# RWKV attention and a top-1 mixture of experts in one kernel: the start of the first chunk, and when the first experts' weights are loaded and split

## Chip, cores and metric

The kernel runs on one core of a Trainium2 chip. The metric is the device time of one execution in microseconds (us); three runs of the kernel before took 287.07, 287.21 and 288.65 us.

## What is computed

```python
# attention: 4 batches, 8 heads, 768 tokens, 48 elements a head
for t in range(S):
    kv = einsum('bhd,bhe->bhde', kt, vt)
    y[:, :, t] = einsum('bhd,bhde->bhe', rt, state + u[None, :, :, None] * kv)
    state = wt[..., None] * state + kv
x = y as (3072 tokens, 384)
# experts: 8 of them, 384 -> 1024 -> 384, each token goes to one
skip = x @ w_skip > 0            # which tokens are computed at all
e = argmax(x @ w_gate)           # its expert, gate = softmax weight of that expert
out = x + gate * (relu(x @ w1[e]) @ w2[e])     # for the tokens computed, else x
```

All is float32; matrix products in the expert part are made of two parts per weight, a high part (rounded, "h") and a low part (the weight less the high part, "l").

## The kernel before

**Attention.** The 4 x 768 tokens are 24 chunks of 128 tokens. One loop, `for s in range(-2, n + 1)` (L672), is software-pipelined: step s loads chunk s+4 (`load_chunk`, L168), loads the transposed and the plain v of chunk s+3 (`load_turned`, `load_v`), stores the rows of chunk s-1, prepares chunk s+2, makes the scores of chunk s+1 and the outputs of chunk s. The buffers `wrk_sb` hold w, r and k of a chunk, three of them in turn.

Preparing a chunk: `prep_scan` (L300) makes q, a reverse running product of w, on VectorE (DVE); `prep_keys` (L322) a reciprocal on DVE and kq = k q on GpSimd (POOL); `prep_reads` (L328) a forward scan rh on DVE and rp = r rh, on POOL but for chunk 0, where DVE does it (L335). `bonus_keys` (L317) makes rk = r k on POOL, for chunk 0 at the end of step -2. The scan of rh takes its start values from a table, `reads_w`, that DVE builds at L261. `scores` (L353) are TensorE (PE) matmuls of kq and rp into two PSUM banks psA; `mask` (L362) multiplies them by a triangle into asb on DVE; `outputs` (L405, L409) multiply asb by v. `fill` (L666) issues matmuls on constant data whose result nobody reads, 11 before the loop, 4 at step -1 and 3 at step 0.

In the start, the memsets and small copies to PSUM zeros, to the gate matrices `wgp` and to `ubk` are issued by `setup` (L238), on ScalarE (ACT) and POOL.

**Queues.** All loads and stores of the loop are issued by SyncE (SP) in program order. A DMA signals one of eight semaphores, taken in turn over all DMAs of SyncE and ScalarE; a DMA waits until the DMA eight places earlier, whose semaphore it takes, has landed.

**Experts' weights.** `load_weights(e, q)` (L75) loads the first (q = 0) or second (q = 1) weights of expert e in three DMAs of 512 KB into a buffer of one of two tags. Expert 1's first and second weights and expert 0's second take turns in one of them, `r1`. Splitting a slice of 512 columns is a copy to the high part on ACT and a subtraction for the low part, on POOL (`split_high`, L100, whose subtraction is issued behind the next rp) or on DVE (`split_slice`, L91). In the loop, `parts` and `gens` (L671, L749) say when: expert 0's second weights are loaded at steps 5, 6 and 7 and split from step 7 on, expert 1's first loaded at steps 16 to 18 and split from step 18 on, most of them after step 21; expert 0's first at steps 19 to 21, used unsplit.

**After the loop.** `early_expert` (L639) runs the first 128 tokens of expert 0; h0l is the low part of its hidden layer. `expert(e)` (L853) does the rest of expert 0 and then experts 1 to 7, 256 tokens at most each: hidden layer psH, hh (high part, ACT), hl (low part, DVE), products psO with w2h and w2l, then fin. Between the activations it splits the next expert's weights, one slice at a time (`more`). `tokens` gathers the tokens of the next expert and makes xTh and xTl of them. The second weights of expert 1 (`r_11`) are loaded when the buffer of its first is read to the end.

## Time and profile before

| | us |
|---|---|
| median of the runs (287.07, 287.21, 288.65) | 287.21 |
| the profiled execution | 286.06 |
| its span in the profile | 284.2 |
| PE busy | 271.2 |
| DVE busy | 217.0 |
| ACT busy | 159.4 |
| POOL busy | 145.9 |

The span runs from the first to the last instruction of the trace; the execution's time has 1.86 us more around it. Busy shares are means over stages with different limits, so the rows below are read by stretch. In a row of the timeline the bracket at the end gives how long the engine stood idle before it and what it waited for.

### The profile page before, as it was taken

The numbers are of one execution on the slowest core, as the hardware profiler recorded it, in microseconds if no ns is written. First come the engines' busy times: TensorE is split into PE (matmuls) and PEld (weight loads), VectorE is DVE, ScalarE is ACT, GpSimd is POOL, SyncE is SP. The second block draws the span as 40 slices with busy tenths as digits, with TensorE's granted clock in tenths as the row PEclk, the third lists the DMA queues.
The fourth block names the chain that finished last, engine by engine and source line by source line (L and its number), as shares of the span: only waits on it lengthen the run. The fifth ranks groups of instructions, "written<-read, shape, count | busy, mean of one in ns | idle before, by whom it ended". The sixth has DMA issues, their size and how long they took to land.

```text
span 284.2 us, 8967 instructions
## 1 busy us (share of the span) xinstructions
PE 271.2 (95%) x3601; PEld 248.9 (88%) x3602; DVE 217.0 (76%) x414; ACT 159.4 (56%) x464; POOL 145.9 (51%) x140
## 2 busy tenths in 40 slices
PE   6998999999999999999999999999999999999993
PEld 2687878788887888887999999999999999999992
DVE  7997999999989999972747697948859588595320
ACT  5175555787658957768416573827638276381310
POOL 4986775699978998974656625011030110201111
PEclk9999999999999999999999999999999999999999
DMA  7999999998999869992078997565672656700001
GB/s 217 239 311 333 277 345 339 363 332 246 297 278 302 252 218 348 308 310 65 28 256 294 345 314 267 212 213 200 221 258 68 231 200 221 268 5 28 10 5 41
DMA packets 26131, 64.41 MB, mean 227 GB/s; under 512 B 4342, under 2 KB 15386, under 8 KB 26080
## 3 DMA queue, kind: packets, MB, share of 16 engines
q1 hardware_dynamic: 23712, 58.14, 62.3%
q0 software_dynamic: 2048, 5.48, 5.9%
q8 instruction: 30, 0.49, 0.7%
q10 hardware_dynamic: 320, 0.13, 0.2%
q14 instruction: 21, 0.17, 0.2%
HBM read 56.69 MB, written 7.86 MB: 227 GB/s over the span
## 4 chain that ended last, share of the span: by engine, by line
PE 57%; POOL 8%; issue 6%; DVE 4%; ACT 3%; DMA 1%; POOLq 0%; DVEq 0%; ACTq 0%
PE psH L884 7%; PE psH L883 7%; PE psH L882 7%; PE psO L906 6%; PE psO L908 6%; PE psO L907 6%; PE psH L133 4%; PE psY L409 3%; POOL rp L336 2%; PE psA L358 2%; POOL kq L326 2%; PE psY L413 2%; PE psX L815 2%; PE psO L658 2%; PE psX L425 1%
## 5 line engine op out<-in xcount | busy, mean ns | idle before, releaser
L820 POOL DMA_INDIRECT out<-fin,ids x16 | 16.8, 1047 | 99.1 <-DVE fin L915 92.7
L889 ACT ACTIVATE hh<-psH 128x256 fp32r<-128x256 f32 x60 | 23.1, 385 | 56.6 <-PE psH L884 53.4
L884 PE MATMUL psH<-xTh,w1l 128*128 128x256 f32 x168 | 47.5, 283 | 0.0
L883 PE MATMUL psH<-xTl,w1h 128*128 128x256 f32 x168 | 47.5, 283 | 0.0
L882 PE MATMUL psH<-xTh,w1h 128*128 128x256 f32 x168 | 47.5, 283 | 0.0
L906 PE MATMUL psO<-w2h,hh 128*128 128x384 f32 x120 | 40.9, 341 | 0.0
L908 PE MATMUL psO<-w2h,hl 128*128 128x384 f32 x120 | 40.2, 335 | 0.0
L907 PE MATMUL psO<-w2l,hh 128*128 128x384 f32 x120 | 40.1, 335 | 0.0
L894 DVE SCALAR_TENSOR_TENSOR hl<-psH,hh 128x256 fp32r<-128x256 f32 x60 | 25.1, 418 | 13.3 <-ACT hh L889 12.0
L326 POOL TENSOR_TENSOR kq<-wrk,q 128x512 f32<-128x512 f32 x24 | 28.2, 1177 | 11.7 <-DVE q L309 3.5
L364 DVE TENSOR_TENSOR asb<-psA,c_sb 128x512 f32<-128x512 f32 x48 | 30.4, 676 | 3.5 <-PE psA L358 3.4
L331 DVE TENSOR_TENSOR_SCAN rh<-wrk,rowsk,pss 128x520 f32<-128x520 f32 x24 | 31.1, 1296 | 2.0
L318 POOL TENSOR_TENSOR rk<-wrk 128x512 f32<-128x512 f32 x24 | 31.0, 1292 | 2.4 <-DMA wrk<-wrk 2.4
L884 PEld LDWEIGHTS psH<-xTh,w1l 128*128 128x128 f32 x168 | 32.2, 192 | 0.0
L883 PEld LDWEIGHTS psH<-xTl,w1h 128*128 128x128 f32 x168 | 32.2, 192 | 0.0
L882 PEld LDWEIGHTS psH<-xTh,w1h 128*128 128x128 f32 x168 | 32.2, 191 | 0.0
L309 DVE TENSOR_TENSOR_SCAN q<-wrk,pss 128x520 f32<-128x520 f32 x24 | 29.5, 1230 | 3.0 <-DMA wrk<-wrk 0.9
L336 POOL TENSOR_TENSOR rp<-wrk,rh 128x512 f32<-128x512 f32 x23 | 27.2, 1181 | 5.4 <-DVE rh L331 5.0
L89 DVE TENSOR_TENSOR w2l<-r,w2h 128x512 fp32r<-128x512 f32 x42 | 27.7, 685 | 2.0 <-ACT w2h L88 1.4
L409 PE MATMUL psY<-asb,v 128*48 128x128 f32 x384 | 26.5, 276 | 2.6 <-DVE psY L381 2.3
L915 DVE SCALAR_TENSOR_TENSOR fin<-psO,gates,xg 128x384 f32<-128x384 f32 x15 | 9.3, 618 | 25.2 <-PE psO L908 24.6
L358 PE MATMUL psA<-rp,kq 64*64 64x128 f32 (+1 forms) x768 | 26.0, 251 | 1.8 <-issue 1.1
(154 smaller groups left out, 608.4 us busy)
## 6 DMA issues: line engine op xcount, KB each, us to landing
r<-w SPq DMA_DIRECT2D x48, 512.0 KB
wrk<-wrk SPq DMA_DIRECT2D x21, 772.5 KB
v<-vN SPq DMA_DIRECT2D x24, 192.0 KB
vt<-wrk SPq DMA_DIRECT2D x48, 96.0 KB
out<-x SPq DMA_DIRECT2D x24, 192.0 KB
wrk<-wrk SPq DMA_DIRECT2D x1, 579.4 KB
wrk<-wrk SPq DMA_DIRECT2D x1, 512.0 KB
wrk<-wrk SPq DMA_DIRECT2D x1, 384.0 KB
```

Of the source, the lines that this page charges most:

```text
L318: nc.gpsimd.tensor_tensor(work[i]["rk"].rearrange("p a j -> p (a j)"), t[:, R_OFF:K_OFF], t[:, K_OFF:V_OFF], op=ALU.mult)
L326: nc.gpsimd.tensor_tensor(kq, wk["k"], wk["q"][:, :, 1:1 + P], op=ALU.mult)
L331: nc.vector.tensor_tensor_scan(rh.rearrange("p a j -> p (a j)"), wk["w"][:, 0:NP * CW], reads_at[:, :NP * CW], rowsk, op0=ALU.mult, op1=AL ...
L336: eng.tensor_tensor(rp, wk["r"], rh[:, :, :P], op=ALU.mult)
L358: nc.tensor.matmul(psa[g][j:j + HP, a, j:], wk["kq"][rows, a, j:j + HP], wk["rp"][rows, a, j:], start=True, stop=True)
L409: nc.tensor.matmul(y_at(a, g), v[:, 2 * a + g], wk["asb"][g][:, a], start=False, stop=True, skip_group_check=True)
L882: nc.tensor.matmul(ps, w1h[:, o:o + P], xTh[:, kc], start=(kc == 0), stop=False)
L883: nc.tensor.matmul(ps, w1h[:, o:o + P], xTl[:, kc], start=False, stop=False)
L884: nc.tensor.matmul(ps, w1l[:, o:o + P], xTh[:, kc], start=False, stop=(kc == KC - 1))
L906: nc.tensor.matmul(pso, h[j, fc][0], w2h[:, o], start=(fc == 0), stop=False)
L907: nc.tensor.matmul(pso, h[j, fc][0], w2l[:, o], start=False, stop=False)
L908: nc.tensor.matmul(pso, h[j, fc][1], w2h[:, o], start=False, stop=(fc == FC - 1))
```

## The change

Chunk 0's transfer of r and k is made in two, k first. Its rp goes from DVE to POOL, and rk of chunks 0 and 1 behind rp. The table of the reads is made by ACT, the constants that ACT spreads come behind it, in a function of their own, after chunk 0's first preparation. Seven of the matmuls that only fill become two. All weights are loaded in six pieces of 512 columns (256 KB). Expert 0's second weights come one piece at a time in six steps, and are split in six named steps; expert 1's first weights are loaded in steps 22 to 24 and split after the loop, their low parts on DVE.

```diff
@@ load_weights
-        for i in range(3):
-            o = i * 1024
-            yield nc.sync.dma_start(wr[:, o:o + 1024],
-                                    w12[e, :, q * KC * DF + o:q * KC * DF + o + 1024])
+        for i in range(6):
+            o = i * 512
+            yield nc.sync.dma_start(wr[:, o:o + 512],
+                                    w12[e, :, q * KC * DF + o:q * KC * DF + o + 512])
@@ load_chunk, i == 0
-                nc.sync.dma_start(t[KO:LO, R_OFF:V_OFF], rows[:2 * D, R_OFF:V_OFF])
+                nc.sync.dma_start(t[KO:LO, K_OFF:V_OFF], rows[:2 * D, K_OFF:V_OFF])
+                nc.sync.dma_start(t[KO:LO, R_OFF:K_OFF], rows[:2 * D, R_OFF:K_OFF])
@@ setup
-            nc.vector.tensor_scalar(reads_w.bitcast(U32), ints, rowsk, None, op0=ALU.mult)
...
+        def spread_constants():
             for z in psa:
                 nc.scalar.copy(z.rearrange("p a j -> p (a j)"), warm)
...
             nc.scalar.copy(ubk_sb, u_sb.rearrange("p (a o) -> p a o", o=1).to_broadcast([P, NP, D]))
@@ prep_scan
-            if i > 0:
+            if i == 0:
+                nc.scalar.activation(reads_w.bitcast(U32), ones_w.bitcast(U32), AF.Copy, scale=rowsk)
+            if i > 1:
                 bonus_keys(i)
@@ prep_reads
-            eng = nc.gpsimd if i > 0 else nc.vector
-            eng.tensor_tensor(rp, wk["r"], rh[:, :, :P], op=ALU.mult)
+            nc.gpsimd.tensor_tensor(rp, wk["r"], rh[:, :, :P], op=ALU.mult)
+            if i <= 1:
+                bonus_keys(i)
@@ the loop
-            parts = [(4, 0, i) for i in range(6, 12)] + [(15, 1, 0)] + [(19, 1, i) for i in range(1, 6)]
+            fetch = {5: (0, 1), 6: (0, 1), 8: (0, 1), 9: (0, 1), 13: (0, 1), 15: (0, 1)}
+            fetch.update({t: (0, 0) for t in (19, 20, 21)})
+            fetch.update({t: (1, 0) for t in (22, 23, 24)})
+            parts = {t: 6 + i for i, t in enumerate((7, 11, 12, 13, 18, 21))}
...
-                    if s == 0:
-                        fill(3)
...
+                if s == -2:
+                    spread_constants()
...
                 if s == -2:
-                    bonus_keys(0)
-                    nc.gpsimd.memset(vt_sb[3], 0.0)
+                    nc.scalar.copy(vt_sb[3].rearrange("p o j -> p (o j)"), warm)
+                if s == -1:
...
-                        fill(4)
+                        fill(2)
...
+                if s in fetch:
+                    eq = fetch[s]
+                    if eq not in gens:
                         gens[eq] = load_weights(*eq)
+                    for _ in range(1 if eq == (0, 1) else 2):
                         next(gens[eq])
+                if s in parts:
+                    split_high(0, parts[s])
@@ after the loop, ahead of expert 0's remainder
-            early_low(1)
+            early_low(2)
+            for i in range(3):
+                split_slice(1, i)
             for k in range(done[0], 6 * FC - 4):
                 next(todo)
             early_tokens(1)
+            for i in range(3, 6):
+                split_slice(1, i)
```

Lines behind the edits have other numbers in the changed kernel (L336 is L338, L318 is L321, L161 is L160, L84 is L83, L89 is L88, L894 is L901). POOL's order at the start, from its last memset of `setup` to rp of chunk 1, before (L717 to L720 are memsets; wrk_88 and wrk_89 are chunks 0 and 1):

```order
L266 MEMSET wgp_sb 128x420
L326 ISA
L326 TENSOR_TENSOR kq_182<-wrk_88,q_178 128x512
L318 TENSOR_TENSOR rk_180<-wrk_88 128x512
L717 MEMSET vt_94 128x512
L718 MEMSET onesb 128x128
L719 MEMSET ohs 128x8
L720 MEMSET key 128x54
L318 TENSOR_TENSOR rk_206<-wrk_89 128x512
L326 TENSOR_TENSOR kq_209<-wrk_89,q_204 128x512
L336 TENSOR_TENSOR rp_213<-wrk_89,rh_211 128x512
```

The same stretch in the changed kernel:

```order
L263 MEMSET wgp_sb 128x420
L329 ISA
L329 TENSOR_TENSOR kq_183<-wrk_88,q_171 128x512
L338 TENSOR_TENSOR rp_187<-wrk_88,rh_185 128x512
L321 TENSOR_TENSOR rk_173<-wrk_88 128x512
L329 TENSOR_TENSOR kq_206<-wrk_89,q_202 128x512
L338 TENSOR_TENSOR rp_210<-wrk_89,rh_208 128x512
L321 TENSOR_TENSOR rk_204<-wrk_89 128x512
```

rp of chunk 0 is new on POOL; rk of chunks 0 and 1 stands behind rp, and the memsets behind both chunks.

SyncE's order at the start, from the second part of chunk 1's load to the load of chunk 2 (wrk_90), with the semaphores waited for (DMAHW0 to 7 are the eight), before:

```order
L180 DMA wrk_89<-wrk 128x1024
L185 DMA v_137<-vN 128x384 [waits DMAHW0_49]
L161 DMA vt_91<-wrk 48x2x256 [waits DMAHW1_49,Pool_49]
L161 DMA vt_91<-wrk 48x2x256 [waits DMAHW2_49]
L180 DMA wrk_90<-wrk 128x1545 [waits DMAHW3_49]
```

And in the changed kernel:

```order
L180 DMA wrk_89<-wrk 128x521
L180 DMA wrk_89<-wrk 128x1024 [waits DMAHW0_49]
L185 DMA v_138<-vN 128x384 [waits DMAHW1_49]
L160 DMA vt_91<-wrk 48x2x256 [waits DMAHW2_49,Pool_49]
L160 DMA vt_91<-wrk 48x2x256 [waits DMAHW3_49]
L180 DMA wrk_90<-wrk 128x1545 [waits DMAHW4_49]
```

With one DMA more in front, each takes the semaphore of the next in the row: the second transposed load of v now waits for DMAHW3 (the second of three small copies of u on ScalarE's queue), for which the load of chunk 2 waited before.

DVE's order between the low parts of the early expert and the first low part of expert 0's remainder (hl_0), in the changed kernel; before, the six rows of w1l are not there, and gates follows h0l:

```order
L640 TENSOR_TENSOR h0l<-hf_2634,h0h 128x512
L640 TENSOR_TENSOR h0l<-hf_2693,h0h 128x512
L88 TENSOR_TENSOR w1l_1_2710<-r_10_2548,w1h_1_2709 128x512 [waits DMAHW7_49,Activation_49]
L88 TENSOR_TENSOR w1l_1_2710<-r_10_2548,w1h_1_2709 128x512 [waits DMAHW0_49,Activation_49]
L88 TENSOR_TENSOR w1l_1_2710<-r_10_2548,w1h_1_2709 128x512 [waits DMAHW2_49,Activation_49]
L88 TENSOR_TENSOR w1l_1_2710<-r_10_2548,w1h_1_2709 128x512 [waits DMAHW3_49,Activation_49]
L88 TENSOR_TENSOR w1l_1_2710<-r_10_2548,w1h_1_2709 128x512 [waits DMAHW5_49,Activation_49]
L88 TENSOR_TENSOR w1l_1_2710<-r_10_2548,w1h_1_2709 128x512 [waits DMAHW6_49,Activation_49]
L790 TENSOR_REDUCE gates<-pss 128x16 [waits PE_49]
L901 SCALAR_TENSOR_TENSOR hl_0_2799<-psH_0_2797,hh_0_2798 128x256 [waits DMAHW4_49,DMAHW1_49,Activation_49]
```

SyncE's order at the end of the attention, from the last load of expert 0's first weights (r_00) to the first load of expert 1's second weights (r_11), before:

```order
L84 DMA r_00_2259<-w 128x1024 [waits DMAHW1_49]
L435 DMA out<-x_2478 128x384 [waits DMAHW2_49,Activation_49]
L435 DMA out<-x_2558 128x384 [waits DMAHW3_49,Activation_49]
L435 DMA out<-x_2594 128x384 [waits DMAHW4_49,Activation_49]
L84 DMA r_11_2760<-w 128x1024 [waits DMAHW5_49,DMASW1_49,Pool_49]
```

And in the changed kernel, from the fourth piece of expert 1's first weights (r_10) on:

```order
L83 DMA r_10_2548<-w 128x512 [waits DMAHW3_49]
L439 DMA out<-x_2586 128x384 [waits DMAHW4_49,Activation_49]
L83 DMA r_10_2548<-w 128x512 [waits DMAHW5_49]
L83 DMA r_10_2548<-w 128x512 [waits DMAHW6_49]
L83 DMA r_11_2764<-w 128x512 [waits DMAHW3_49,DMAHW5_49,DMAHW2_49,DMAHW6_49,DMAHW0_49,DMAHW7_49,DMASW1_49,DVE_49]
```

The first load of r_11 waited for POOL, which had read the last of expert 1's first weights there; it now waits for DVE, which reads them in the six rows of w1l.

## Rows read from the trace of the kernel before

**Rows 1.** The page, part 1: busy time, share of the span and instructions.

```profile
PE 271.2 (95%) x3601; PEld 248.9 (88%) x3602; DVE 217.0 (76%) x414; ACT 159.4 (56%) x464; POOL 145.9 (51%) x140
```

**Rows 2.** Busy time by stretch; the first line names the columns.

```profile
core 0: us, PE busy (x) PEld busy (x) DVE busy (x) ACT busy (x) POOL busy (x), PEclk, DMA share, GB/s
8.00:14.00 6.00, 5.68 (x105) 3.94 (x109) 5.90 (x9) 0.96 (x4) 6.00 (x9) 1.00 0.94 229
...
24.00:60.00 36.00, 34.01 (x707) 29.17 (x705) 33.10 (x56) 22.37 (x82) 25.96 (x23) 1.00 1.03 329
...
84.00:106.00 22.00, 20.62 (x445) 17.80 (x442) 20.66 (x36) 16.19 (x55) 21.25 (x20) 1.00 0.83 256
...
127.00:152.00 25.00, 24.48 (x290) 22.62 (x287) 12.72 (x39) 12.51 (x34) 14.08 (x13) 1.00 0.40 138
152.00:266.00 114.00, 114.00 (x817) 113.72 (x816) 83.13 (x165) 62.71 (x140) 24.56 (x23) 1.00 0.58 203
```

**Rows 3.** Timeline, DVE at the start: start us, us, engine, line, operation, tiles.

```profile
3.52 0.36 DVE L261 TENSOR_SCALAR pss<-pss,rowsk 128x131 uint32<-128x131 uint32 x1
4.00 1.24 DVE L309 TENSOR_TENSOR_SCAN q<-wrk,pss 128x520 f32<-128x520 f32 x1
...
5.49 1.30 DVE L331 TENSOR_TENSOR_SCAN rh<-wrk,rowsk,pss 128x520 f32<-128x520 f32 x1
6.82 1.30 DVE L336 TENSOR_TENSOR rp<-wrk,rh 128x512 f32<-128x512 f32 x1
8.04 1.22 DVE L309 TENSOR_TENSOR_SCAN q<-wrk,pss 128x520 f32<-128x520 f32 x1
...
10.73 1.26 DVE L364 TENSOR_TENSOR asb<-psA,c_sb 128x512 f32<-128x512 f32 x2
...
12.59 1.24 DVE L309 TENSOR_TENSOR_SCAN q<-wrk,pss 128x520 f32<-128x520 f32 x1
...
17.31 1.24 DVE L309 TENSOR_TENSOR_SCAN q<-wrk,pss 128x520 f32<-128x520 f32 x1
...
22.87 1.24 DVE L309 TENSOR_TENSOR_SCAN q<-wrk,pss 128x520 f32<-128x520 f32 x1 [0.93 <-DMA wrk<-wrk]
```

**Rows 4.** Timeline, POOL at the start: kq of chunk 0, rp of chunk 1, rk of chunk 3.

```profile
6.40 1.17 POOL L326 TENSOR_TENSOR kq<-wrk,q 128x512 f32<-128x512 f32 x1 [3.37 <-DMA wrk<-wrk]
...
12.31 1.18 POOL L336 TENSOR_TENSOR rp<-wrk,rh 128x512 f32<-128x512 f32 x1
...
17.34 1.27 POOL L318 TENSOR_TENSOR rk<-wrk 128x512 f32<-128x512 f32 x1 [0.35 <-DMA wrk<-wrk]
```

**Rows 5.** Timeline, SyncE's issues of the loads of chunks 2 and 3.

```profile
5.98 0.35 SPq L180 DMA_DIRECT2D wrk<-wrk  x1
...
12.54 0.35 SPq L180 DMA_DIRECT2D wrk<-wrk  x1
```

**Rows 6.** Groups by line, POOL from 23 to 127 us: low parts, count, busy us, mean ns.

```profile
L107 POOL TENSOR_TENSOR w2l<-r,w2h 128x512 fp32r<-128x512 f32 x6 | 7.6, 1273 | 0.0
```

**Rows 7.** Waits of DVE (8 to 127 us) and PE (8 to 152): total us, times, longest.

```profile
DVE asb L364 <- PE psA L358: 1.1, 3, 0.5
DVE q L309 <- DMA wrk<-wrk: 0.9, 1, 0.9
```

```profile
PE psA L358 <- issue: 1.1, 1, 1.1
...
PE psA L358 <- POOL rp L336: 0.3, 1, 0.3
```

**Rows 8.** The page, part 5: low parts on DVE among the experts.

```profile
L89 DVE TENSOR_TENSOR w2l<-r,w2h 128x512 fp32r<-128x512 f32 x42 | 27.7, 685 | 2.0 <-ACT w2h L88 1.4
```

**Rows 9.** Timeline, the handover: DVE's and ACT's rows, then PE's, then SyncE's load.

```profile
142.84 1.29 DVE L636 TENSOR_TENSOR h0l<-hf,h0h 128x512 fp32r<-128x512 f32 x2
...
147.93 0.42 DVE L894 SCALAR_TENSOR_TENSOR hl<-psH,hh 128x256 fp32r<-128x256 f32 x1 [1.26 <-DMA r<-w]
...
153.22 1.01 DVE L89 TENSOR_TENSOR xTl<-psX,xTh 128x384 fp32r<-128x384 f32 x2
...
142.16 0.21 ACT L574 CAST vals<-pss 128x6 bf16<-128x6 f32 x1
144.91 0.48 ACT L629 COPY xT<-psX 128x384 f32<-128x384 f32 x1 [2.54 <-PE psX L628]
147.51 0.38 ACT L889 ACTIVATE hh<-psH 128x256 fp32r<-128x256 f32 x1 [2.12 <-DMA r<-w]
149.12 0.62 ACT L88 CAST w2h<-r 128x512 fp32r<-128x512 f32 x1 [1.22 <-DMA r<-w]
...
151.78 0.42 PE L906 MATMUL psO<-w2h,hh 128*128 128x384 f32 x1
...
156.15 0.28 PE L883 MATMUL psH<-xTl,w1h 128*128 128x256 f32 x1
...
143.82 13.05 SPq L84 DMA_DIRECT2D r<-w  x9
```

More of the change, by code (lines that the diff above doesn't have):

```diff
@@ L273, in setup @@
             nc.scalar.copy(ubk_sb, u_sb.rearrange("p (a o) -> p a o", o=1).to_broadcast([P, NP, D]))
-            for g in range(2):
-                nc.tensor.matmul(psy2[:, g].rearrange("p s j -> p (s j)"), warm[:, :P], warm,
-                                 start=True, stop=True, skip_group_check=True)
-            nc.tensor.matmul(psu.rearrange("p a j -> p (a j)"), warm[:, :P], warm[:, :NP * HP],
-                             start=True, stop=True, skip_group_check=True)
         later, held, marks, ending = deque(), [], deque(), []
```

20 lines of the change are left out of this document (7 added, 13 removed).

## The prediction

> **What bounds the kernel now.** I read the page's busy shares first, then the table by stretch, then the start of the program instruction by instruction, then the waits of the middle, and last the place where the attention steps hand over to the experts. The page names TensorE (PE) as the busiest engine, 271.2 of 284.2 us [rows 1], but that is an average over unlike stages. The table by stretch [rows 2] shows them: from 152 to 266 us PE is busy 114.00 of 114.00 us, so what is late at 152 is late at the end, and nothing before it is made good there. Between 24 and 106 VectorE (DVE) has almost no slack (33.10 of 36 and 20.66 of 22 us), GpSimd (POOL) is full only from 84 to 106 (21.25 of 22), and the DMA engines are saturated from 8 to 60 (shares 0.94 to 1.03). So there are three questions: when the first steps get their data, who paces the middle, and whether the handover to expert 1 stays hidden.
>
> **The start.** In the rows of DVE [rows 3] look at what stands between the scan q of chunk 0 and asb of chunk 0 at 10.73. The change takes two instructions out of it: the table (0.36 us) and the product rp (1.30 us). It moves the first to ScalarE, which is idle there, and the second to POOL. q of chunk 0 can't start much earlier than 4.00, since its weights must land, so the table is worth 0.1 us at most. After the reciprocal and rh end at 6.78, q of chunk 1 starts at 6.8 instead of 8.04 and asb of chunk 0 at 10.73 - 1.2 = 9.5 to 9.6. PE's scores must be there by then: now kq starts at 6.40, after 3.37 us of waiting for r and k in one transfer [rows 4]. With k first, kq starts when q ends, near 5.3, and ends near 6.5; rp on POOL follows rh, 6.8 to 8.0 by the usual 1.18 us. DVE's rp ended at 8.12. The scores therefore start within 0.2 us of where they do, asb can begin at 9.6, and the first outputs come **1.1 us earlier** (1.66 us at the very most, both instructions whole).
>
> That gain does not survive the next loads. q of chunk 2 starts at 12.59 [rows 3], 0.05 us after the load of chunk 3 was issued at 12.54 [rows 5]; that issue waits for the landing of chunk 2's load (its buffer is another one; the wait is for the DMA eight issues earlier), so chunk 2 had landed just before. POOL waits for chunk 3's landing until 17.34 [rows 4] and q of chunk 3 starts at 17.31; q of chunk 4 waits 0.93 us for its own load, until 22.87 [rows 3]. Three loads in a row are the clock of this stretch, and the DMA engines are saturated from 8 us on [rows 2]. The change doesn't issue them earlier: chunk 2's load is behind one DMA more, and the second transposed v load ahead of it on SyncE's queue now waits for a later one of the eight (the second small copy of u, which landed just before 5.98; before, that wait stood at chunk 2's own load [rows 5]). So it is issued at 6.0 to 6.5 instead of 5.98. The queue is full then, so I take 0 for it and +0.4 as the bad end. The good end is the whole 1.1 us, if chunk 4's load moves with chunk 3's. **Front: 0, from -1.1 to +0.4.** The zero is covered by the loads; DVE waits longer at q of chunk 2 and of chunk 4 instead.
>
> Five fill matmuls go. They run on PE between its scores and the outputs, where PE waits anyway, 5.68 of 6.00 us busy from 8 to 14 [rows 2] with fills counted: 0.
>
> **The middle.** Six low parts of expert 0's second weights run on POOL, 1.27 us each [rows 6]; they move to other steps, two fewer before 106 us. POOL is full from 84 to 106, so up to 2 x 1.27 = 2.5 us could come back if POOL set the pace. But DVE is idle there only 22.00 - 20.66 = 1.34 us [rows 2], and the whole middle has one PE wait for rp on POOL, 0.3 us [rows 7]. DVE's waits for PE's scores are 1.1 us in three places, all of it behind one 1.1 us stall of PE of which the trace shows no cause but "issue" [rows 7]; nothing says it goes. I take **-0.4, from 0 to -1.3**: the one wait for POOL and a little more, between nothing and DVE's whole idle time there. The weights that move to later steps relieve the DMA queue; DVE waits 0.9 us in all of 8 to 127 for a chunk's load, at q of chunk 4 [rows 7], before any of them: 0. The new copies of the first ScalarE steps lie in its idle time: 0.
>
> **The handover.** Expert 1's first weights are loaded late now, in steps 22 to 24, and split after the steps: six casts on ScalarE, six low parts on DVE, 0.685 us each by the same kind of instruction on DVE [rows 8], 4.1 us in all. DVE is idle for this (12.72 of 25 us busy from 127 to 152 [rows 2]), and so is ScalarE between 142.37 and 147.51 but for one copy [rows 9]. The low parts follow h0l, which ends at 144.13, and alternate with casts; the last ends near 148.0. The first hl of expert 0's remainder is due at 147.93 and barely feels it. What does feel it is on SyncE. The load of expert 1's second weights takes the buffer that those six read, so it waits for the last of them: issue at **148.0 instead of 143.82** [rows 9]. ScalarE's queue has a cast of that load (w2h) between the activations hh 0 and hh 1, and it already waits for the landing now, until 149.12 [rows 9], 5.3 us after the issue of 512 KB.
>
> For a piece of 256 KB there is no row. Upper bound: 5.3 less the 256 KB saved at the 329 GB/s of 24 to 60 us [rows 2], 0.8, so 4.5. Lower bound: chunk 3's load, issued at 12.54 and used at 17.34 [rows 4, 5], is 4.8 us for 772 KB; less 516 KB at the same rate, 1.6, that is 3.2. I take the middle, 3.85: landing near 151.85. From the start of that cast to the end of xTl (ScalarE alternates casts and activations, then both xTh, then DVE's xTl) the trace has 154.23 - 149.12 = 5.1 us [rows 9], which gives 156.95. PE asks for xTl at 156.15 [rows 9], and runs without a gap until then. **Handover: +0.8, from +0.2** (landing 3.2 us after the issue) **to +1.5** (4.5 us). The loads of expert 2 come behind it by up to 2 us; PE's work on expert 1 (some 14 us, about an eighth of the 114) covers that.
>
> The six pieces hold for all weights, 48 loads of 512 KB become 96 of 256 KB. From 152 to 266 the queue is 0.58 busy [rows 2] and PE never waits: 0. The Trainium skill, DMA: Bandwidth & Descriptors, section Bandwidth, says to batch DMAs to 1 MiB or more for three quarters of peak, which speaks against halving them; by it the transfers of the experts would cost more, but no row here shows PE waiting for them, so by the rule too the sum stays, and only the rival of the pieces, below, gains.
>
> **Sum.** 0 - 0.4 + 0.8 = +0.4 us on the profiled execution's 286.06, so 286.5. That execution lies 1.15 us under the median of the runs, 287.21; with the same distance the forecast is **287.6**, a difference of 0.14%, inside the 0.5% (1.4 us) that a measurement of this kernel can tell. The ends of the terms add up to -2.2 and +1.9.
>
> **Rivals.**
> - *The front's gain lives on.* If the loads of chunks 2 to 4 follow the earlier steps, because chunk 4's issue moves up with the buffers, 1.1 us come through and with POOL's relief 0.3 to 1.3 more: 287.6 - 1.1 - 0.5 = 286.0, down to 285.0 where the handover costs little. For it: DVE's work shrinks by 1.66 us. Against: the 0.93 us wait for the load of chunk 4. Chance 0.17.
> - *POOL is the pace from 60 to 106.* The chain of POOL work there would shrink by 2.5 us and DVE's idle time with it: 287.6 - 2.1 (the 0.4 is in the forecast already) = 285.5, and 284.9 with a cheap handover. For it: 21.25 of 22 us busy. Against: only 0.3 us of PE's waits end at POOL. Chance 0.10.
> - *The handover breaks: slower.* The mechanism is the single wait at expert 1's second weights. If the gathers of expert tokens, which run at the same time, hold the first piece back as long as the 512 KB before (5.3 us) or longer, it lands after 153.3, the cast holds hh 1 to hh 3 in ScalarE's queue, PE first stops at the products of hh 1 (due near 152.8, six matmuls of 0.17 us behind the first at 151.78 [rows 9]) and again at xTl: a landing at 153.3 gives 153.3 + 5.1 - 156.15 = 2.25 us instead of 0.8, and with no relief in the middle 289.4. It decides at a landing of 152.8, where the stall passes 1.7 us and the total 0.5%. Chance 0.18.
> - *The pieces cost by themselves.* Twice the DMAs wait for each other through the eight semaphores, the casts of an expert come late once per expert, 0.3 us for seven experts: 287.6 + 2.1 = 289.7. For it: issues at the start already wait for a DMA eight places earlier (chunk 3's at 12.54 [rows 5]); against: the share 0.58 and PE's full stretch. Chance 0.03. The rule of the Trainium skill above points the same way.
> - *The clock falls without the fills.* The granted clock is 1.00 in every stretch [rows 2], 2.4 GHz; at 1.2 GHz PE's 5.7 busy us of 8 to 14 would double and 3 to 6 us be lost, 291 to 294. Chance 0.02.
> - *My forecast*, loads cover the front and the handover costs some tenths: 0.50.
>
> **How the numbers follow.** The first two rivals give 0.27; of that 0.23 lies under 285.8, with 0.02 from the low end of the forecast's own bounds: faster 0.25. The three slower ones give 0.23, of which 0.03 stays within 0.5%: slower 0.20. The rest, 0.55, is no difference to be told. For 8 in 10 the range has to reach the usual outcome of both main rivals: 285.2 to 289.1. Predicted: 287.6, the likeliest case.
>
> **What would show it.** Right: in the changed profile asb of chunk 0 starts near 9.6 and the first outputs near 11.6, but q of chunk 2 still near 12.6, q of chunk 4 near 22.9 with a wait for its load of over 1 us; the middle keeps DVE near 33 of 36 us; SyncE issues expert 1's second weights near 148, ScalarE's first cast of them starts near 151.9 and PE has a gap under 1.5 us ahead of expert 1. Wrong: q of chunk 4 before 22.3 (the front lives on), a step of 60 to 106 shorter by over 0.1 us (POOL was the pace), the first cast after 152.8 (the handover breaks), or gaps of PE inside 160 to 266 (the pieces).

## The result, and the profile after

| us | before | after |
|---|---|---|
| median (lowest to highest, 8 runs each) | 287.12 (285.83 to 288.65) | 290.37 (288.92 to 290.86) |
| ratio of after to before, 95% interval | | 1.0102 (1.0074 to 1.0130) |
| the profiled execution / its span | 286.06 / 284.2 | 290.35 / 288.5 |

The changed kernel is 1.0% slower. The forecast was 287.6, range 285.2 to 289.1, with a chance of 0.20 that it would be slower: wrong.

The difference of the two spans, 4.27 us, falls into six stretches whose borders are starts of named instructions in the two traces:

| stretch, us | before | after | difference | predicted |
|---|---|---|---|---|
| to the scan q of chunk 6 | 32.74 | 33.73 | +1.0 | 0 |
| q of chunk 6 to q of chunk 23 | 88.35 | 87.80 | -0.55 | -0.4 |
| q of chunk 23 to the first product psO with hh of expert 0's remainder | 30.69 | 30.34 | -0.35 | 0 |
| from there to the first matmul with xTl of expert 1 (**the handover**) | 4.37 | 7.06 | +2.7 | +0.8 |
| from there to the last fin | 123.22 | 123.33 | +0.1 | 0 |
| the last fin to the end of the span | 4.84 | 6.22 | +1.4 | not in the sum |

The table by stretch of after; its columns are those of [rows 2], and its first four lines stand for the same stretches as the first four there:

```profile
8.00:14.00 6.00, 5.19 (x116) 3.95 (x118) 4.37 (x7) 1.87 (x8) 5.38 (x9) 1.00 0.91 248
24.00:60.00 36.00, 34.62 (x735) 30.25 (x737) 33.70 (x57) 21.69 (x80) 26.11 (x22) 1.00 1.02 325
84.00:106.00 22.00, 21.04 (x459) 18.42 (x458) 20.77 (x36) 15.09 (x52) 20.75 (x21) 1.00 0.94 292
127.00:152.00 25.00, 24.32 (x296) 22.84 (x297) 13.96 (x43) 11.36 (x30) 8.31 (x8) 1.00 0.51 155
152.00:170.00 18.00, 16.01 (x115) 15.12 (x114) 14.57 (x30) 12.51 (x29) 10.90 (x10) 1.00 1.00 358
170.00:266.00 96.00, 96.00 (x681) 95.72 (x680) 70.03 (x138) 51.48 (x113) 14.08 (x13) 1.00 0.55 184
```

PE, full from 152 to 266 before [rows 2], now has two idle microseconds from 152 to 170, and is full from 170 on: what is lost at the handover is not made good. The granted clock is 1.00 in each of these stretches, the level of 2.4 GHz.

**The start.** DVE's timeline of after, to be read beside [rows 3], and then POOL's beside [rows 4]:

```profile
3.91 1.24 DVE L310 TENSOR_TENSOR_SCAN q<-wrk,pss 128x520 f32<-128x520 f32 x1 [0.43 <-DMA wrk<-wrk]
...
7.62 1.24 DVE L310 TENSOR_TENSOR_SCAN q<-wrk,pss 128x520 f32<-128x520 f32 x1 [0.76 <-DMA wrk<-wrk]
...
10.32 1.26 DVE L368 TENSOR_TENSOR asb<-psA,c_sb 128x512 f32<-128x512 f32 x2
...
13.74 1.24 DVE L310 TENSOR_TENSOR_SCAN q<-wrk,pss 128x520 f32<-128x520 f32 x1 [1.55 <-DMA wrk<-wrk]
19.77 1.24 DVE L310 TENSOR_TENSOR_SCAN q<-wrk,pss 128x520 f32<-128x520 f32 x1 [1.38 <-DMA wrk<-wrk]
...
24.32 1.23 DVE L310 TENSOR_TENSOR_SCAN q<-wrk,pss 128x520 f32<-128x520 f32 x1
```

```profile
5.26 1.17 POOL L329 TENSOR_TENSOR kq<-wrk,q 128x512 f32<-128x512 f32 x1 [2.22 <-DVE q L310]
6.94 1.18 POOL L338 TENSOR_TENSOR rp<-wrk,rh 128x512 f32<-128x512 f32 x1 [0.51 <-DVE rh L334]
```

kq and rp of chunk 0 are where the prediction put them. asb is 0.4 us earlier, not 1.1, because q of chunk 1 has a wait of its own for its load, up to 7.62, which in before lay under rp. Then q of chunks 2 and 3 wait for their loads; q of chunk 4 is 1.5 us later than before. The load of chunk 2 was not issued late (SyncE's timeline of after; before it was 5.98 [rows 5]), it took longer, until q of chunk 2 at 13.74 instead of 12.59:

```profile
5.73 0.52 SPq L180 DMA_DIRECT2D wrk<-wrk  x1
```

**The middle.** Two of its steps are shorter. These are q of chunks 12 and 13, before and then after:

```profile
63.65 1.23 DVE L309 TENSOR_TENSOR_SCAN q<-wrk,pss 128x520 f32<-128x520 f32 x1
...
68.37 1.23 DVE L309 TENSOR_TENSOR_SCAN q<-wrk,pss 128x520 f32<-128x520 f32 x1
```

```profile
64.41 1.23 DVE L310 TENSOR_TENSOR_SCAN q<-wrk,pss 128x520 f32<-128x520 f32 x1
...
68.95 1.23 DVE L310 TENSOR_TENSOR_SCAN q<-wrk,pss 128x520 f32<-128x520 f32 x1
```

From chunk 12 to 13, and again from 18 to 19, every kernel on record with before's weights takes 4.71 to 4.72 us and every one with the new weights 4.54 to 4.55. That is 0.34 us in all. The other 0.2 us of the -0.55 lie in the first step, from chunk 6 to 7, which takes 4.88 to 5.93 us in kernels of either kind: it depends on how the start ended.

**Ahead of the experts.** The 0.35 us are at `hot`, six comparisons on DVE after the last step. In before POOL splits w1l beside them (POOL's timeline, then DVE's):

```profile
134.80 3.73 POOL L107 TENSOR_TENSOR w1l<-r,w1h 128x512 fp32r<-128x512 f32 x3 [0.59 <-ACT w1h L106]
...
137.58 2.00 DVE L528 TENSOR_SCALAR hot<-iota,rall 128x256 bf16<-128x256 bf16 x6
```

and in after POOL is idle there:

```profile
137.94 1.27 DVE L532 TENSOR_SCALAR hot<-iota,rall 128x256 bf16<-128x256 bf16 x6
```

2.00 us against 1.27 for the same six instructions: in before the first of them takes 1.03 us and ends as the last low part beside it ends, at 138.5 to 138.6, the others take 0.27 us as in after (0.28). The Trainium skill, SBUF — State Buffer, section Who interferes with whom, says that a DVE tensor_scalar can take the port pair that DVE shares with GpSimd for the length of the instruction, and that the one that comes second is blocked; the rows agree. Every kernel below that keeps w1l off POOL has 30.3 to 30.5 us in this stretch, the others 30.7.

**The handover.** ACT, DVE and PE in the timeline of after, then SyncE's issue of the load; [rows 9] answer to them:

```profile
147.60 0.38 ACT L896 ACTIVATE hh<-psH 128x256 fp32r<-128x256 f32 x1 [0.56 <-ACT w1h L87]
150.69 0.62 ACT L87 CAST w2h<-r 128x512 fp32r<-128x512 f32 x1 [2.70 <-DMA r<-w]
151.22 0.38 ACT L896 ACTIVATE hh<-psH 128x256 fp32r<-128x256 f32 x1
154.70 0.62 ACT L87 CAST w2h<-r 128x512 fp32r<-128x512 f32 x1 [3.10 <-DMA r<-w]
155.22 0.38 ACT L896 ACTIVATE hh<-psH 128x256 fp32r<-128x256 f32 x1
...
144.14 3.80 DVE L88 TENSOR_TENSOR w1l<-r,w1h 128x512 fp32r<-128x512 f32 x6
...
157.87 1.01 DVE L88 TENSOR_TENSOR xTl<-psX,xTh 128x384 fp32r<-128x384 f32 x2
...
151.87 0.42 PE L913 MATMUL psO<-w2h,hh 128*128 128x384 f32 x1
...
155.65 0.44 PE L913 MATMUL psO<-w2h,hh 128*128 128x384 f32 x1 [1.45 <-ACT hh L896]
...
158.93 0.38 PE L890 MATMUL psH<-xTl,w1h 128*128 128x256 f32 x1 [0.37 <-DVE xTl L88]
...
147.96 13.42 SPq L83 DMA_DIRECT2D r<-w  x15
```

The six low parts on DVE and the issue at 147.96 are as predicted (144.1, 148.0). The first piece is there at 150.7, earlier than the 151.85 I took. The second, issued 0.4 us behind the first, is cast at 154.70, four microseconds after the first. That cast stands in ACT's queue ahead of an activation hh, and PE waits 1.45 us for that hh and again for xTl. What runs beside the load are the gathers of expert 2's tokens, in POOL's timeline of after:

```profile
146.17 1.43 POOL L446 DMA_INDIRECT xg<-out,idr  x1 [1.68 <-DVE w1l L88]
147.91 1.00 POOL L446 DMA_INDIRECT xg<-out,idr  x1 [0.30 <-issue]
```

Before, they started at 146.07 and 147.38, behind the issue of the load at 143.82 [rows 9]. The view by line has the spread for the six pieces issued from 147.9 to 150.7 (us from issue to landing):

```profile
DMA to landing us min/median/max: 2.7/6.6/7.6
```

**The end.** The trace of DVE's sequencer has 633 instructions instead of 587; 42 of the 46 more are separate waits (210 against 168), because six pieces of a weight have six semaphores where three had three. Behind the last fin DVE has six instructions left in both kernels. The third last, a wait in the handshake of all engines that ends the program, begins 4.19 us after that fin in before and 5.88 us in after. Only DVE is late there: ACT and PE (PEld is PE's queue of weight loads) pass the same handshake 4.3 us after the fin. After, by line, from 286 to 288.2 us:

```profile
L1101 ACTq EVENT_SEMAPHORE  x1: 17/17/17, 286.5 to 286.5; - x1
L1101 PEldq EVENT_SEMAPHORE  x1: 51/51/51, 286.5 to 286.5; - x1
...
L1101 DVEq EVENT_SEMAPHORE  x1: 21/21/21, 288.1 to 288.1; - x1
```

The DMA view from the last fin to 290 us has one more read of instructions in after. Before (queue, kind, packets, MB, share of the engines):

```profile
q14 instruction: 4, 0.03, 1.1%
```

and after:

```profile
q14 instruction: 5, 0.04, 1.9%
```

The fifth read goes with the late end, but DVE can't have waited for it: in the same view up to 288.1 us, where the late instruction begins, after has four too. For which read DVE waited, or whether for one at all, is not shown.

```profile
q14 instruction: 4, 0.03, 2.0%
```

### The profile page after: what moved, and what is told of

Its sections match the earlier page's. It is cut to its first block, busy times and chain, and to the rows that moved or that the text cites. A ratio compares the mean times of both kernels' runs of the same rounds, so it can differ in the third digit from the quotient of the medians.

```text
span 288.5 us, 9044 instructions
## 1 busy us (share of the span) xinstructions
PE 269.5 (93%) x3597; PEld 248.3 (86%) x3597; DVE 218.5 (76%) x418; ACT 161.3 (56%) x466; POOL 139.6 (48%) x134
## 4 chain that ended last, share of the span: by engine, by line
issue 34%; PE 8%; POOL 6%; DVE 4%; DMA 2%; ACT 2%; POOLq 1%; SPq 0%; DVEq 0%; ACTq 0%
POOL out L827 5%; DMA r<-w 2%; PE psH L132 2%; PE psY L413 1%; PE psH L890 1%; DVE w1l L88 1%; DVE w2l L88 1%; PE psH L891 1%; PE psH L889 1%; ACT w2h L87 1%; PE psA L362 1%; PE psY L417 1%; DVE xTl L88 0%; POOLq L929 0%; POOL kq L329 0%
## 5 line engine op out<-in xcount | busy, mean ns | idle before, releaser
L901 DVE SCALAR_TENSOR_TENSOR hl<-psH,hh 128x256 fp32r<-128x256 f32 x60 | 25.2, 420 | 9.8 <-ACT hh L896 9.8
L338 POOL TENSOR_TENSOR rp<-wrk,rh 128x512 f32<-128x512 f32 x24 | 28.5, 1186 | 8.0 <-DVE rh L334 8.0
L88 DVE TENSOR_TENSOR w2l<-r,w2h 128x512 fp32r<-128x512 f32 x42 | 27.8, 688 | 5.7 <-ACT w2h L87 5.1
L321 POOL TENSOR_TENSOR rk<-wrk 128x512 f32<-128x512 f32 x24 | 30.7, 1280 | 2.3 <-DMA wrk<-wrk 2.3
L88 DVE TENSOR_TENSOR w1l<-r,w1h 128x512 fp32r<-128x512 f32 x42 | 28.7, 692 | 2.1 <-DMA r<-w 0.2
L422 ACT COPY xT<-psY 128x512 f32<-128x512 f32 x24 | 14.1, 587 | 25.7 <-PE psY L417 20.9
```

What stands on the lines that cost most here:

```text
L88: (eng or nc.vector).tensor_tensor(dst_l, src, dst_h.bitcast(F32), op=ALU.subtract)
L321: nc.gpsimd.tensor_tensor(work[i]["rk"].rearrange("p a j -> p (a j)"), t[:, R_OFF:K_OFF], t[:, K_OFF:V_OFF], op=ALU.mult)
```

## The experiments

Theories, with the forecast behind them wrong by 2.8 us: the second weights of expert 1 come late piece by piece because the gathers of expert 2's tokens use the DMA engines at the same time (rival: the pieces are too small); the program's end is late because DVE's last instructions moved behind the border of a block that must still be read (rival: the end hangs on something else); the start costs about 1 us (rival: it costs nothing, and loads scatter by that much). All runs in one table: medians, the ratio to before measured beside them on the same chip, and from each profile the handover, the time from the last fin to the end, and q of chunk 6. Medians of different groups are from different chips or hours, and before's own median beside them lies between 286.65 and 288.44; compare the ratios.

| run | median | ratio (95%) | handover | end | q of chunk 6 |
|---|---|---|---|---|---|
| e1_front | 287.73 | 1.0043 (1.0009 to 1.0078) | 4.37 | 5.04 | 33.39 |
| e2_weights | 290.68 | 1.0120 (1.0075 to 1.0165) | 6.03 | 6.55 | 33.12 |
| e3_one_rk | 291.44 | 1.0161 (1.0106 to 1.0217) | 7.12 | 5.95 | 34.53 |
| e4_gather_later | 293.16 | 1.0234 (1.0188 to 1.0280) | 5.08 | 5.97 | 33.34 |
| e5_pad | 288.92 | 1.0037 (0.9996 to 1.0079) | 7.39 | 4.86 | 33.96 |
| e6_before_pad4 | 287.22 | 0.9988 (0.9948 to 1.0029) | 4.37 | 4.90 | 31.89 |
| e7_casts_behind | 288.54 | 1.0061 (1.0039 to 1.0083) | 4.36 | 5.79 | 33.96 |
| e8_weights_mended | 287.44 | 0.9996 (0.9963 to 1.0029) | 4.37 | 5.09 | 32.83 |
| e9_carried | 286.11 | 0.9910 (0.9881 to 0.9938) | 4.37 | 5.02 | 33.29 |
| f1_front_order | 288.62 | 1.0038 (0.9998 to 1.0078) | 4.37 | 5.00 | 33.82 |
| f2_transfers | 288.50 | 1.0009 (0.9974 to 1.0043) | 4.37 | 5.00 | 33.80 |
| e10_three_pieces | 289.76 | 1.0052 (1.0017 to 1.0086) | 7.36 | 5.99 | 33.21 |
| g1_carried_front | 285.98 | 0.9984 (0.9962 to 1.0007) | 4.37 | 4.90 | 33.13 |
| g2_carried_order | 285.71 | 0.9962 (0.9929 to 0.9995) | 4.37 | 4.81 | 33.42 |
| g3_carried_transfers | 286.28 | 0.9983 (0.9958 to 1.0009) | 4.37 | 4.97 | 34.07 |
| g4_carried_no_pad | 287.99 | 1.0031 (1.0004 to 1.0057) | 4.37 | 6.78 | 33.21 |
| h1_carried_again | 285.80 | 0.9937 (0.9904 to 0.9970) | 4.37 | 5.07 | 33.33 |
| h2_carried_front_again | 286.14 | 0.9947 (0.9916 to 0.9977) | 4.37 | 5.04 | 33.20 |

**The two halves of the change.** e1 keeps before's weights (loads, splits, pieces of 512 KB) and has the new start; e2 keeps before's start and has the new weights.

> Only the start of the change: chunk 0's transfer in two, rp on GpSimd, the table and the constants on ScalarE, fewer fills; all weights as in the kernel before. Theory A (two separate losses: the first loads land later and the handover to expert 1 stalls): chunk 2's load still lands near 13.6 us instead of 12.5, q of chunk 5 starts near 28.9 instead of 27.9, no gap of PE before expert 1, total about 1.0 us over the kernel before (288.1). Theory B (the start costs nothing that lasts, all of the loss comes from the weights): q of chunk 5 near 27.9 and a total within 0.3 us of the kernel before.

> Only the weights' part of the change, with the start of the kernel before. Theory A: q of chunk 5 at 27.9, the steps after it some 0.5 us shorter in all than in the kernel before, PE's gap ahead of expert 1 again about 2.5 us, total 1.8 us over the kernel before (288.9). Theory B: the whole 3.2 us over the kernel before (290.3).

e2 is as slow as the whole change, and has both late stretches, the handover and the end. The weights half is the cause of the loss; the start adds at most what e1 shows, 0.55 us by the medians, between its two theories.

**The handover: who holds the second piece?** e4 issues the gathers of expert 2's tokens later, behind the fourth activation:

```diff
-        pair(2)
-        later_pairs = list(range(3, E))
+        later_pairs = list(range(2, E))
...
-                if later_pairs and (e, q) != (0, 0):
+                if later_pairs and (e > 0 or q > 2):
```

> The changed kernel, but the gathers of expert 2's tokens wait for the fourth activation of expert 0's remainder, so that no gather runs beside the first loads of expert 1's second weights. Theory C (the gathers, which now run at the same time, hold the second piece back): the second piece lands within 1.5 us of the first instead of 4.0, PE's gap ahead of expert 1 is under 1 us, total 2 us under the changed kernel (288.3). Theory D (the later issue and the smaller pieces alone do it): the second piece still lands 3 to 4 us behind the first, total unchanged (290.4).

ACT's casts of the six pieces in e4:

```profile
150.62 0.62 ACT L87 CAST w2h<-r 128x512 fp32r<-128x512 f32 x1 [3.04 <-DMA r<-w]
...
151.43 0.61 ACT L87 CAST w2h<-r 128x512 fp32r<-128x512 f32 x1
```

The first piece comes as in after, the second with no wait at all 0.8 us behind it: the gathers are what held it. (In e2, e3 and e5, where the gathers run beside the load as in after, the second cast starts 2.6 to 3.8 us behind the first.) The time is nevertheless worse than that of the changed kernel, by 1.3%: the gathers now run until 171.6 beside the loads of the next weights, and PE, full in before, waits among the experts (waits of PE from 148 to 288):

```profile
PE psO L912 <- ACT hh L895: 1.4, 1, 1.4
PE psO L913 <- issue: 1.0, 1, 1.0
```

From the first xTl to the last fin it takes 129.09 us instead of 123.33. The delay was moved, not removed; that the later gathers cause just these waits was not followed further. The waits are also not the whole loss: behind them the granted clock falls to the level of 1.2 GHz for part of 174 to 180 us (columns of [rows 2]):

```profile
172.00:174.00 2.00, 0.61 (x4) 0.40 (x3) 0.50 (x2) 1.00 (x3) 0.00 (x0) 1.00 1.00 299
174.00:176.00 2.00, 2.00 (x8) 2.00 (x8) 2.00 (x4) 2.00 (x5) 0.00 (x0) 0.57 0.71 280
```

e10 changes the size instead, three pieces of 512 KB for this one load:

```diff
-        for i in range(6):
-            o = i * 512
+        k = 3 if (e, q) == (1, 1) else 6
+        for i in range(k):
+            m = KC * DF // k
+            o = i * m
```

> The changed kernel, with expert 1's second weights alone loaded in three pieces of 512 KB instead of six of 256 KB, issued at the same moment (about 148.0). Theory that the small pieces are what delays the handover (the second came 4.0 us after the first): handover under 6 us (7.06 in the changed kernel), time 289 or less. Theory that the late issue beside the gathers of expert 2's tokens does it, whatever the size: first landing near 153, since 512 KB took 5.3 us in before, handover 6.5 to 8 us, time 290 to 291.

The first cast starts at 151.86, the next that waits at 155.63, and the handover takes 7.36 us: the size is not it. (The time is below that of the changed kernel, but the two intervals overlap.) The Trainium skill, DMA: Bandwidth & Descriptors, section Bandwidth, would have the larger pieces do better by its batching rule; the handover shows no such gain. The Trainium skill, DMA: Bandwidth & Descriptors, section SWDGE vs HWDGE vs iDMA, says that GpSimd's transfers and SyncE's lie in different queues of the same engines, which take turns between them; e4 agrees as far as the sharing goes, 0.8 us between the two pieces without the gathers and 4.0 with them.

e7 leaves gathers and pieces alone and takes the casts out of the way: ACT and DVE split nothing between the activations of expert 0's remainder, the six slices come behind them.

```diff
-                more(1)
+                if e > 0:
+                    more(1)
```

> The changed kernel, but the splits of expert 1's second weights stand behind the four activations of expert 0's remainder and behind its tokens, on ScalarE and on DVE, so that no activation waits for the landing. Theory H (the loss of the handover is the queue on ScalarE behind the cast that waits): from the first product with hh to the first with xTl 4.4 us as before instead of 7.1, total 2.6 us under the changed kernel (287.8). Theory I (the late loads themselves are the bound): PE stops as long at expert 1's products with its second weights, total within 0.7 us of the changed kernel.

The handover is 4.36 us, that of before, though the pieces are late as they were (the cast of the sixth waits for it until 158.34). So the loss was not the late landing as such but the activations queued behind a cast that waited for it. The time falls by less than expected (288.54, and not 287.8), because a part of the loss moved on: six low parts in a row stand on DVE ahead of the first hl of expert 1 (waits of PE in e7 from 148 to 284):

```profile
PE psH L889 <- DVE hl L901: 1.0, 1, 1.0
```

**The end.** e6 puts four one-element memsets on DVE into before, e5 sixteen into the changed kernel, all after the last step:

```diff
+                if s == n:
+                    spare = keep.tile([P, 1], F32, name="spare")
+                    for _ in range(16):
+                        nc.vector.memset(spare[:1], 0.0)
```

> The kernel before with 4 memsets of one element on DVE behind the last step: as many DVE instructions as the changed kernel has. Theory F: the end takes 6.2 us instead of 4.8, total 1.4 us over the kernel before (288.6). Theory G: the end and the total as in the kernel before, within 0.3 us.

> The changed kernel with 16 memsets of one element on DVE behind the last step, where it has gaps. In the changed kernel the time from the start of the last fin to the end of the span is 6.2 us, before 4.8, and one of DVE's last instructions starts 1.5 us late behind a read of instructions. Theory F (four more DVE instructions put the last ones of the program into another block that has to be read first): with 16 more the block's border lies where DVE waits anyway, the end takes 4.8 to 5.0 us, total 1.4 us under the changed kernel (289.0). Theory G (the end is longer for another reason, as the last scatter or the many small transfers): it stays 6.2 us, total unchanged (290.4).

e6 missed: I had counted four more instructions for the change, and it is 46, so four more in before say nothing of the theory. e5 hit: with sixteen instructions more the end is 4.86 us instead of 6.22, the reads in the DMA view are back at four, and the time falls by 1.4 us (the intervals of the two ratios just touch), though its own handover came out worse (7.39).

```profile
q14 instruction: 4, 0.03, 1.7%
```

The granted clock may have a part in that: behind PE's wait it falls to 0.50, the level of 1.2 GHz, where the profiled execution of after keeps 1.00 behind the same wait. It need not be the whole, for e10 has 7.36 at 1.00. Here is e5, in the columns of [rows 2]:

```profile
155.00:157.00 2.00, 0.78 (x3) 0.46 (x4) 1.25 (x3) 1.90 (x5) 0.73 (x1) 1.00 1.08 418
...
158.00:160.00 2.00, 2.00 (x8) 2.00 (x8) 2.00 (x5) 1.16 (x3) 1.62 (x2) 0.50 1.04 379
```

**Both mended.** e8 is before's start, the weights half, the casts behind and the sixteen fillers. e9 adds that the slices not yet split are carried into the next expert's activations:

```diff
-                todo = list(range(0 if e > 0 else 6, 12))
+                todo = [(e + 1, i) for i in range(0 if e > 0 else 6, 12)]
+            todo = carried + todo
+            carried.clear()
...
+            if e + 1 < E:
+                carried.extend(todo)
+                todo.clear()
             more(12)
             if e + 2 < E:
                 drain(load_weights(e + 2, 0))
-                drain(load_weights(e + 2, 1))
+                pending.append((e + 2, 1))
```

The pending load is issued behind the sixth activation, when the carried slices have been read.

> The start of the kernel before, the weights' part of the change, the splits behind the activations, and 16 one-element memsets. If the gains of the middle (0.4 us) and of the hot columns without GpSimd's low parts (0.35 us) are real and both losses are mended: 286.4 to 286.6, 0.2 to 0.3% under the kernel before. If the gains were of one profile only: 287.2. If either loss has another cause: 288.5 and more.

> The kernel of the run e8_weights_mended (287.44 us: start of before, the weights part, the splits of expert 1's second weights behind the activations, sixteen one-element fillers), with one change: of the next expert's second-weight slices only as many are split as the own activations have room for, and the rest are carried into the next expert's loop, one behind each activation; the loads that take their buffer are issued after them. If the one stall that e8 has left (PE waits 1.0 us for hl of expert 1, behind six low parts in a row on DVE) is what cancels the gain of the middle, the handover stays 4.4 us (first psO to first psH of expert 1), the time from the first xTl matmul to the last fin falls from 124.4 to 123.3, and the time comes to about 286.4, under before (287.2) and under the changed kernel (290.4). Rival: the carried slices are late for their own products, or the loads behind them are late for the next expert: the stall only moves, 287.4 or more.

e8 is as fast as before: PE's one wait of 1.0 us for hl eats the gain of the middle. e9 has no PE wait at all from 148 to 282, 123.13 us from the first xTl to the last fin, and is faster than before, by 0.9% here and 0.6% in the repetition h1 (the changed kernel is 1.0% slower than before). Its stretches account for 0.6 us of that (0.34 in the middle, 0.2 at `hot`, 0.1 among the experts), and its profiled span is only 0.1 us under that of before, with a later start and end. The rest, 1.2 to 2.0 us, is that before's runs beside it lie higher and wider (285.5 to 290.5 us beside h1, whose own are 285.0 to 286.8) than its profiled one, and why they do is open. So the size of the gain is open too: g1, g2 and g3 below, which are e9 with the new start or a part of it, lie 0.2 to 0.4% under before on another chip. g4 is e9 without the fillers, 634 instructions on DVE instead of 650:

> As e9_carried (286.1 us, 650 instructions executed by DVE, 4.96 us from the last fin to the end) without the sixteen one-element fillers, so 634 instructions. Theory that the late read of a block of instructions decides the end: near 6.4 us from the last fin to the end, an instruction of DVE's last four begins over 1 us late, and the time is 287.5, 1.4 us longer although sixteen instructions are gone. Rival (the end is tied to something else than DVE's count): 5.0 us and 286.1.

Again five reads instead of four, an end of 6.78 us instead of 5.02, and a time above before: sixteen instructions fewer cost 1.8 us at the end, and g4 is 1.7 us above g3 on the same chip. The rival, that the end hangs on something else than DVE's count, falls; why the count matters is not shown.

```profile
q14 instruction: 5, 0.04, 1.3%
```

**The start.** e3 is the changed kernel with r and k of chunk 0 in one transfer; f1 and f2 put the order of work alone, and the extra transfer alone, into before; g1, g2 and g3 put the whole, the order and the transfer on top of e9. The edit of the transfer, as in f2:

```diff
-                nc.sync.dma_start(t[KO:LO, R_OFF:V_OFF], rows[:2 * D, R_OFF:V_OFF])
+                nc.sync.dma_start(t[KO:LO, K_OFF:V_OFF], rows[:2 * D, K_OFF:V_OFF])
+                nc.sync.dma_start(t[KO:LO, R_OFF:K_OFF], rows[:2 * D, R_OFF:K_OFF])
```

> The changed kernel, but r and k of chunk 0 in one transfer of 4 KB rows as before. Theory A1 (the loss of the start is the third transfer, which puts every load behind it half a microsecond later on SyncE and reads 2 KB rows): chunk 1's r and k land near 8.4 instead of 9.5, chunk 2 near 12.5 instead of 13.6, q of chunk 5 near 27.9 or earlier, total 1 us under the changed kernel. Theory A2 (the loss comes from the new order on GpSimd and ScalarE, which frees buffers later): loads land as in the changed kernel and the total stays within 0.3 us of it.

> Before, with only the changed order of work at the start: table by ScalarE, rp of chunk 0 on GpSimd, rk behind rp, constants later, two fill matmuls for seven; r and k of chunk 0 stay in one transfer and the weights part is left as before. Theory that the order of work makes the start late (GpSimd's longer queue, DVE's instructions earlier against the loads): q of chunk 2 near 13.7 and q of chunk 6 near 33.7, the time 288.2 as in e1_front or slower. Theory that the extra transfer makes it late (one DMA more in the ring of eight, so each load of the first steps is issued behind another landing): q of chunk 2 near 12.9, q of chunk 6 near 32.7, the time 287.2 or, with the earlier asb of chunk 0, up to 1 us less.

> Before, with only the transfer of r and k of chunk 0 made in two, k first; all else as before. Theory that the extra transfer makes the start late: q of chunk 2 near 13.7, q of chunk 6 near 33.7, the time 288.2. Theory that the order of work does it: q of chunk 2 near 12.9, q of chunk 6 near 32.7, the time 287.2.

> The kernel of the run e9_carried (286.1 us, its runs within 285.5 to 286.7) with the whole front part of the change added: k first, rp on GpSimd, table by ScalarE, constants later. Theory that the front part costs about 1 us in any setting (profiles: q of chunk 6 at 32.8 us on average over five kernels with the old start, at 33.7 over seven with the new): 287.1, q of chunk 6 near 33.8. Rival, my forecast of zero for the front (the loads of chunks 2 to 4 cover it, the difference seen so far is scatter of the loads): 286.1, within 0.4 us.

> As g1_carried_front, but r and k of chunk 0 in one transfer, so only the order of work of the start is changed against e9_carried (286.1 us). If the order of work is what costs: 287.1 as g1_carried_front. If the transfers: 286.1. If both act together only: between.

> As e9_carried (286.1 us) with r and k of chunk 0 in two transfers, k first, and nothing else of the front part. If the transfers are what costs: 287.1 and the load of chunk 2 landed near 13.6 us instead of 12.6. If the order of work: 286.1.

e3 starts no earlier than the changed kernel, so the extra transfer alone does not seem to be what makes the start late, though the loads scatter by as much (below). f1 and f2 part nothing: both profiles have q of chunk 6 at 33.8, and the intervals overlap. (f1's profile loses more at the end of the attention, where q of chunk 23 waits 1.60 us for its load.) g1 to g3 landed on another chip than e9 and could not be set against it, so both kernels ran once more side by side:

> The kernel of e9_carried once more, to stand beside the kernel with the front part on the same chip. With g4_carried_no_pad (287.99 us) less the 1.8 us that its late end cost (6.78 against 4.96 us), it should lie near 286.2 on that chip: ratio to before 0.991 to 0.998.

> The kernel of g1_carried_front once more, beside h1_carried_again on one chip: the two differ by the front part alone. Theory that the front part costs about 1 us everywhere: 1 us over h1 (ratio to before higher by 0.0035). Theory of zero (the loads of chunks 2 to 4 set q of chunk 6 whatever is done ahead of them, and they scatter by 1 us from run to run): within 0.5 us of h1.

h2 is 0.34 us over h1, the intervals of the two ratios nearly the same. Over the profiles q of chunk 6 lies at 32.9 us on average for the seven kernels with the old start (31.89 to 33.33) and at 33.5 for the eight with the whole new one (33.13 to 33.96). DVE's q rows of h1 show how much of that is the loads' own scatter, with the old start:

```profile
5.45 1.24 DVE L309 TENSOR_TENSOR_SCAN q<-wrk,pss 128x520 f32<-128x520 f32 x1 [1.56 <-DMA wrk<-wrk]
8.89 1.22 DVE L309 TENSOR_TENSOR_SCAN q<-wrk,pss 128x520 f32<-128x520 f32 x1
13.39 1.24 DVE L309 TENSOR_TENSOR_SCAN q<-wrk,pss 128x520 f32<-128x520 f32 x1
19.37 1.24 DVE L309 TENSOR_TENSOR_SCAN q<-wrk,pss 128x520 f32<-128x520 f32 x1 [1.41 <-DMA wrk<-wrk]
```

q of chunk 0 starts 1.45 us later there than in [rows 3], q of chunk 3 2.1 us later, with the same program up to that point. The start therefore costs between 0 and about 1 us, half of one by the profiles and 0.3 to 0.55 by the medians, and which of its two pieces does it stays open. A gain in it is nowhere to be seen.

## Why the prediction was wrong

- **The steps that held.** That the loads of chunks 2 to 4 cover whatever the start gains: yes, and if anything the term was 0 to +1 instead of 0; within it the 1.1 us at asb were 0.4, since q of chunk 1 waits for a load of its own. The middle: -0.4 predicted, -0.55 measured (median of the kernels with the new weights 87.8 us, without them 88.4). That this came out so near is in part luck: 0.34 us of it is the change, in two steps of 0.17 us each, and by the prediction's own sign (a step of 60 to 106 shorter by over 0.1 us) a small piece of its rival "POOL is the pace". No loss from the pieces among the experts: PE is 96.00 of 96 us busy from 170 to 266. No change of the clock in the profiled execution; e5 and e4 show that it can fall behind such a wait. DVE's six low parts and the issue at 148.0: to a tenth.
- **The step that failed: "Handover: +0.8, from +0.2 to +1.5".** The term measured +2.7. I priced the first piece (3.85 us; it took 2.7) and then took "from the start of that cast to the end of xTl" from before, 5.1 us, as if the other five pieces were on time. In before the load was issued at 143.8, 2.3 us ahead of the first gather (146.07), and its first 512 KB, two slices, were there at 149.12; now the load is issued behind that gather and beside the next. The price belonged to the second piece. From its cast at 154.70 to the end of xTl at 158.88 it is 4.2 us; in before it was 4.3, from the second cast at 149.92 to 154.23, so this part of the working held. This is the rival "the handover breaks", with its place, its queue and nearly its price (2.25), but with the second piece held and not the first; it had 0.18.
- **What was missing: the end.** 1.4 us that no term held. The prediction counted the pieces as transfers only, and gave its rival "the pieces cost by themselves" 0.03; each piece is also a semaphore that its reader has to wait for. The pieces did cost, not by the way of that rival but as 42 more waits in DVE's program, which brought the number of its instructions to where the end is late. With sixteen more still (e5, e8, e9) the end is not late, so the cost is one of the count and not of the pieces' own time.
- **What was missing on the good side:** 0.35 us at `hot`, from w1l leaving POOL. The rows were in the trace: six instructions of one shape, the first at 1.03 us beside POOL's w1l and the others at 0.27.
- **The sum as it came:** 2.7 + 1.4 + 0.1 - 0.55 - 0.35 = 3.3, and the medians differ by 3.25. With the start's +1.0 of that one pair of profiles it is 4.3, the difference of the two profiled executions; the execution profiled before lay 1.06 us under its median.

## What to carry to other kernels

Price a load that is moved piece by piece, not by its first piece alone, and look at what else uses the DMA engines between the two; a cast that may wait for a load must not stand in a queue ahead of an activation that PE needs, and in e9 putting it behind the activations costs nothing, as the row of work that piles up is spread over the next loop; in e7 and e8, where it isn't, PE waits 1.0 us for it. Count the waits that smaller pieces add on each engine: they are instructions too. Where a program's end looks longer by over a microsecond with the same last work, add some empty instructions (sixteen here) to the engine that is late and see.

## What the runs showed of the hardware

The time from the last fin to the end is 4.8 to 5.1 us or 5.8 to 6.8 us, and which of them hangs on how many instructions DVE has executed: 586 to 591, 649 and 650 give the short end, 630, 633 and 634 the long one. In every long end DVE alone is late in the closing handshake, at the third last of its instructions with 630 and 633 and at the fourth last with 634. That is the 631st instruction with 633 and with 634 but the 628th with 630 (e10), so a border that stands still at one count does not fit all three. Ahead of these last instructions DVE executes a conditional branch over the general path. The Trainium skill, Runtime: NRT & Kernel Launch, section Instruction fetch mechanics, says that instructions are read ahead in blocks, that the crossing of a border is mostly hidden, and that a branch out of the blocks held forces a read before execution goes on. A late instruction behind the branch would fit the last part; if it is a border that costs here, it is not hidden, with 1.4 us in after and 1.8 us in g4. Neither is shown: no read was seen to end the wait, and that the branch is what uncovers it wasn't tried.

The granted clock fell from 1.00 to 0.50 inside the work in two of the twenty profiles, behind a wait of PE: in e5, where PE had been busy 0.78 of the 2 us from 155 to 157, and in e4, 0.61 of the 2 us from 172 to 174. In after PE was busy 0.55 of the 2 us from 154 to 156, and the clock stayed at 1.00. So the same handover can cost more in one execution than in another.
